# A gated delta rule with an MLP on one core: a list scheduler inside the kernel fixes every engine's order and the PSUM banks

## The chip, the cores and the metric

The kernel runs on one core of a Trainium2 chip. The metric is device time of one execution in microseconds (us), lower is better. The kernel before takes 668.2 us (median of two runs, 665.67 to 670.74).

The engines are named as in the profile: PE is the tensor engine (PEld its weight loads), DVE the vector engine, ACT the scalar engine, POOL GpSimd, SP the sync engine, which here only issues DMAs.

## The reference

Two stages. The first is a recurrence over 768 tokens for 32 pairs of batch and head (4 x 8), with a 48 x 48 state each; the second an MLP over the 3072 resulting tokens.

```python
def _attn_ref(q, k, v, beta, g):
    k_n = k / (np.linalg.norm(k, axis=-1, keepdims=True) + 1e-06)
    state = np.zeros((B, H, D, D))                       # B 4, H 8, D 48
    for t in range(S):                                   # S 768
        y[:, :, t] = g[:, :, t] * np.einsum('bhd,bhde->bhe', q[:, :, t], state)
        v_old = np.einsum('bhde,bhd->bhe', state, k_n[:, :, t])
        state = state + bt[..., None] * np.einsum('bhd,bhe->bhde', k_n[:, :, t], v[:, :, t] - v_old)

def _moe_ref(x, w_in, w_out):                            # x [3072, 384], w_in [384, 2048]
    h = x @ w_in
    g = np.where(h >= 1, h, np.where(h <= -1, 0.0, (h + 1) ** 2 / 4))
    return g @ w_out
```

## The kernel before

The recurrence is done in 24 chain steps of 32 tokens, in 6 groups of four steps. For a group the kernel loads k, q, v and g (64 DMAs of 48 KB), prepares them on POOL (`prep_pair`), builds Gram matrices on PE (`gram_step`), inverts the 32 x 32 triangular ones in two 16 x 16 halves on POOL (`lanes`, 15 serial pairs of instructions between three DVE transposes), joins the halves on PE (`merge_pair`), and then walks the four chain steps, which alone are serial. After the fourth step the tokens of the group go through the MLP: sixteen `mlp_in` of 128 x 512 and four `mlp_out`.

```python
    def lanes(gi):
        bm = bms[gi % 3]
        lt = lan.tile([128, 32, 32], F16, name=f"lt{gi}", tag="lt")
        nc.vector.transpose(out=lt[:].rearrange("p i j -> p (i j)"), in_=_ap(bm, [[1, 32], [64, 32]]))
        lm = lan.tile([128, 2, 16, 16], FP, name=f"lm{gi}", tag="lm")
        nc.gpsimd.tensor_copy(out=lm[:], in_=eye[:])
        for j in range(15):
            ...                                  # two POOL instructions each: tm = lt * lm, lm -= tm
        low = lows[gi % 2]
        nc.gpsimd.tensor_copy(out=_ap(low, [[528, 2], [32, 16], [1, 16]]), in_=lm[:])
        l16 = lan.tile([128, GS, J, 32], F16, name=f"l16{gi}", tag="l16")
        nc.vector.transpose(out=_ap(l16, [[1, 32], [32, 32]]), in_=_ap(low, [[1, 32], [32, 32]]))
        x16 = lan.tile([128, GS, J, 32], F16, name=f"x16{gi}", tag="x16")
        nc.vector.transpose(out=_ap(x16, [[1, 32], [32, 32]]), in_=_ap(low, [[32, 32], [1, 32]]))

    def mlp_in(gi, xt, m):
        hp = psM.tile([128, NT], FP, name=f"hp{gi}_{m}", tag="m")          # one of two PSUM banks
        ...                                                                # three matmuls
        nc.scalar.activation(out=rl[:], in_=hp[:], func=AF.Relu, bias=c_half[:], scale=0.5)
        if m % 2 == 0:
            nc.vector.tensor_tensor(out=mx[:], in0=hp[:], in1=rl[:], op=ALU.max)
            nc.vector.scalar_tensor_tensor(out=gt[:], in0=rl[:], scalar=1.0, in1=mx[:], op0=ALU.min, op1=ALU.mult)
        else:
            nc.gpsimd.tensor_tensor(out=r2[:], in0=rl[:], in1=rl[:], op=ALU.mult)      # the square
            nc.vector.scalar_tensor_tensor(out=gt[:], in0=hp[:], scalar=1.0, in1=r2[:], op0=ALU.max, op1=ALU.min)

    for s in range(NSTEP):                       # the order: program order, handed to the framework's scheduler
        gi = s // GS
        if gi + 1 < NG:
            if s % GS == 0:
                parts = group_parts(gi + 1)      # load and prep / gram / lanes / merge of the next group
            parts[s % GS]()
        xt = chain_step(s)
        n = (len(todo) + (GS - s % GS) - 1) // (GS - s % GS)
        for f in todo[:n]:                       # a quarter of the previous group's MLP
            f()
        todo = todo[n:]
        ...
```

Of the kernel before, what the change touches and what calls it, by code (L numbers as in the profile page):

```python
# [15 lines left out]
def _ap(t, dims, off=0):  # L16

    a = t[:]
    return bass.AP(tensor=a.tensor, offset=a.offset + off, ap=[list(a.ap[0])] + [list(d) for d in dims])


@with_exitstack
def kernel(
# [13 lines left out]
    C = 32  # L37
# [6 lines left out]
    NM = DFF // 128  # L44
    assert D == 48 and H == 8 and B == 4

    const = ctx.enter_context(tc.tile_pool(name="const", bufs=1))
    raw = ctx.enter_context(tc.tile_pool(name="raw", bufs=2))
    prep = ctx.enter_context(tc.tile_pool(name="prep", bufs=2))
    vtp = ctx.enter_context(tc.tile_pool(name="vtp", bufs=4))  # L50
    small = ctx.enter_context(tc.tile_pool(name="small", bufs=2))
    ktp = ctx.enter_context(tc.tile_pool(name="ktp", bufs=8))
    lan = ctx.enter_context(tc.tile_pool(name="lan", bufs=2))
    nwt = ctx.enter_context(tc.tile_pool(name="nwt", bufs=2))
    zfp = ctx.enter_context(tc.tile_pool(name="zfp", bufs=4))
    chn = ctx.enter_context(tc.tile_pool(name="chn", bufs=2))
    xtp = ctx.enter_context(tc.tile_pool(name="xtp", bufs=2))
    mlpt = ctx.enter_context(tc.tile_pool(name="mlpt", bufs=2))
    mlpg = ctx.enter_context(tc.tile_pool(name="mlpg", bufs=28))
    outp = ctx.enter_context(tc.tile_pool(name="outp", bufs=3))  # L60
    psS = ctx.enter_context(tc.tile_pool(name="psS", bufs=1, space=bass.MemoryType.PSUM))
    psN = ctx.enter_context(tc.tile_pool(name="psN", bufs=2, space=bass.MemoryType.PSUM))
    psC = ctx.enter_context(tc.tile_pool(name="psC", bufs=2, space=bass.MemoryType.PSUM))
    psM = ctx.enter_context(tc.tile_pool(name="psM", bufs=2, space=bass.MemoryType.PSUM))


    HS = 4 * S * D
    raws = {}

    def load(s0, n):  # L70

        ts = {}
        for nm, src in (("k", k), ("q", q), ("v", v), ("g", g)):
            t = raw.tile([128, GS, J, D], FP, name=f"r{nm}{s0}", tag=f"raw_{nm}", bufs=2 if nm == "g" else 1)
            ts[nm] = t
        raws[s0] = ts

    def load_part(s0, off, n, names):
        ts = raws[s0]
        for nm, src in (("k", k), ("q", q), ("v", v), ("g", g)):  # L80
            if nm not in names:
                continue
            for h4 in range(4):
                for c in range(off, off + n):
                    a = bass.AP(tensor=src.tensor, offset=src.offset + h4 * S * D + (s0 + c) * C * D,
                                ap=[[D, C], [HS, J], [1, D]])
                    nc.sync.dma_start(out=ts[nm][32 * h4:32 * h4 + 32, c, :, :], in_=a)  # L87


    braw = const.tile([128, NG, C], FP, name="braw")  # L90
    for h4 in range(4):
        for j in range(J):
            a = bass.AP(tensor=beta.tensor, offset=beta.offset + h4 * S + j * 4 * S,
                        ap=[[C, GS], [GS * C, NG], [1, C]])
            nc.sync.dma_start(out=braw[32 * h4 + 4 * j:32 * h4 + 4 * j + 4, :, :], in_=a)  # L95
    load(0, GS)
    load_part(0, 0, 2, "k")
    load_part(0, 0, 2, "qv")

    ones = const.tile([128, 32], FP, name="ones")  # L100
    nc.gpsimd.memset(ones[:], 1.0)
    id32 = const.tile([128, 32], FP, name="id32")
    upf = const.tile([128, 32], F16, name="upf")
    lof = const.tile([128, 32], F16, name="lof")
    for h4 in range(4):
        r = slice(32 * h4, 32 * h4 + 32)
        nc.gpsimd.affine_select(out=id32[r, :], in_=ones[r, :], compare_op=ALU.is_equal, fill=0.0,
                                base=0, pattern=[[-1, 32]], channel_multiplier=1)
        nc.gpsimd.affine_select(out=upf[r, :], in_=ones[r, :], compare_op=ALU.is_gt, fill=0.0,
                                base=0, pattern=[[1, 32]], channel_multiplier=-1)  # L110
        nc.gpsimd.affine_select(out=lof[r, :], in_=ones[r, :], compare_op=ALU.is_gt, fill=0.0,
                                base=0, pattern=[[-1, 32]], channel_multiplier=1)
    i16 = const.tile([128, 32], F16, name="i16")
    nc.gpsimd.tensor_copy(out=i16[:], in_=id32[:])
    two_i = const.tile([128, 16, 32], F16, name="two_i")
    nc.gpsimd.tensor_scalar(out=two_i[:], in0=_ap(id32, [[0, 16], [1, 32]]), scalar1=-2.0, scalar2=None, op0=ALU.mult)
    upmask = const.tile([128, J, 2, 32], F16, name="upmask")
    nc.gpsimd.tensor_copy(out=upmask[:].rearrange("p j a c -> p (j a) c"), in_=_ap(upf, [[0, 2 * J], [1, 32]]))
    c_half = const.tile([128, 1], FP, name="c_half")
    nc.gpsimd.memset(c_half[:], 0.5)  # L120


    bms = []
    for i in range(3):
        t = const.tile([128, GS, J, 2, 32], F16, name=f"bm{i}")
        nc.gpsimd.memset(t[:], 0.0)
        nc.gpsimd.tensor_copy(out=t[:, :, :, 0, :].rearrange("p s j t -> p (s j) t"), in_=_ap(id32, [[0, GS * J], [1, 32]]))
        bms.append(t)

    lows = []  # L130
    for i in range(2):
        t = const.tile([128, 32, 32], F16, name=f"low{i}")
        nc.gpsimd.memset(t[:], 0.0)
        lows.append(t)
    eye = const.tile([128, 2, 16, 16], FP, name="eye")
    nc.gpsimd.memset(eye[:], 0.0)
    nc.gpsimd.memset(_ap(eye, [[256, 2], [17, 16]]), 1.0)
    kqs = []
    for i in range(5):
        t = const.tile([128, 2, J, 2, 64], F16, name=f"kq{i}")  # L140
        nc.gpsimd.memset(t[:], 0.0)
        kqs.append(t)
    i64 = const.tile([128, 64], F16, name="i64")
    for r in range(2):
        nc.gpsimd.affine_select(out=i64[64 * r:64 * r + 64, :], in_=_ap(ones, [[0, 2], [1, 32]])[64 * r:64 * r + 64], compare_op=ALU.is_equal, fill=0.0,
                                base=0, pattern=[[-1, 64]], channel_multiplier=1)

    sb = const.tile([128, NG, J, GS], FP, name="sb")
    bt = const.tile([128, NG, C], FP, name="bt")
    nc.vector.transpose(out=bt[:].rearrange("p a b -> p (a b)"), in_=braw[:].rearrange("p a b -> p (a b)"))  # L150
    nc.scalar.activation(out=sb[:].rearrange("p a b c -> p (a b c)"), in_=bt[:].rearrange("p a b -> p (a b)"), func=AF.Sqrt)

    load_part(0, 2, 2, "kqv")
    load_part(0, 0, 4, "g")


    win = const.tile([128, 3, DFF], F16, name="win")
    wout = const.tile([128, NM, DM], F16, name="wout")

    def load_weights():  # L160
        for h4 in range(4):
            for p0, kt, h2, e0, n in ((0, 0, 0, 0, 32), (0, 1, 0, 32, 16), (16, 1, 1, 0, 16), (0, 2, 1, 16, 32)):
                r0 = (h2 * 4 + h4) * D + e0
                nc.gpsimd.dma_start(out=win[32 * h4 + p0:32 * h4 + p0 + n, kt, :], in_=moe_w_in[r0:r0 + n, :])  # L164
        nc.gpsimd.dma_start(out=wout[:], in_=moe_w_out.rearrange("(m p) n -> p m n", p=128))


    st = {}

    def prep_pair(p):  # L170
        s0 = 2 * p
        gi, off = s0 // GS, s0 % GS
        rw = raws[gi * GS]
        kr = rw["k"][:, off:off + 2]
        sbv = _ap(sb, [[1, 2], [GS, J]], gi * J * GS + off)
        ksq = prep.tile([128, 2, J, D], FP, name=f"ksq{p}", tag="ksq")
        nc.gpsimd.tensor_tensor(out=ksq[:], in0=kr, in1=kr, op=ALU.mult)  # L177
        nsq = small.tile([128, 2, J], FP, name=f"nsq{p}", tag="nsq")
        nc.vector.tensor_reduce(out=nsq[:], in_=ksq[:], axis=AX.X, op=ALU.add)  # L179
        nrm = small.tile([128, 2, J], FP, name=f"nrm{p}", tag="nrm")  # L180
        nc.scalar.activation(out=nrm[:], in_=nsq[:], func=AF.Sqrt)
        nre = small.tile([128, 2, J], FP, name=f"nre{p}", tag="nre")
        nc.vector.tensor_scalar(out=nre[:], in0=nrm[:], scalar1=1e-6, scalar2=None, op0=ALU.add)
        rcp = small.tile([128, 2, J], FP, name=f"rcp{p}", tag="rcp")
        nc.vector.reciprocal(out=rcp[:], in_=nre[:])
        rs = small.tile([128, 2, J], FP, name=f"rs{p}", tag="rs")
        nc.vector.tensor_tensor(out=rs[:], in0=rcp[:], in1=sbv, op=ALU.mult)
        kq = kqs[p % 5]
# [265 lines left out]
```

## Time and profile before

| | before |
|---|---|
| time | 668.2 us |
| period of a group (transpose lt of one group to that of the next, mean of five) | 102 us |
| first chain product / last chain transpose / tail to the end | 81 / 617 / 48 us |
| mean granted PE clock | 0.69 |

The first fence holds two lines of the profile's page: busy time of each engine (with its share of the span), and the engines' shares of the chain of work that ended last.

```profile
PE 317.9 (48%) x7536; PEld 170.3 (26%) x7536; DVE 240.9 (36%) x306; ACT 149.3 (22%) x253; POOL 223.2 (34%) x356
...
issue 27%; POOL 19%; PE 19%; DVE 13%; SPq 12%; ACT 5%; DMA 3%; POOLq 0%; ACTq 0%; DVEq 0%
```

No engine is half busy, and the chain of waits passes from one to another without a favourite. The next fence is the view by stretches of time: start and end, length, then busy us of PE, PEld, DVE, ACT and POOL (with instruction counts), the granted clock of PE, the share of DMA and GB/s. The first stretch is one whole group, the second the part of a later group in which POOL inverts and DVE transposes what comes out.

```profile
350.00:456.00 106.00, 55.17 (x1273) 27.81 (x1272) 39.98 (x52) 24.66 (x42) 31.38 (x50) 0.60 0.19 39
...
460.00:484.00 24.00, 3.75 (x72) 1.43 (x71) 12.19 (x7) 2.65 (x4) 15.79 (x33) 0.50 0.00 0
```

In that part PE works 3.8 of 24 us. The timeline (start, duration, engine, line, operation, output<-inputs, and in brackets how long the engine sat idle before it and what ended that) shows why.

```profile
464.08 1.04 POOL L363 TENSOR_TENSOR r_13_8305<-rl_13_8302 128x512 f32<-128x512 f32 x1
465.16 0.69 DVE L364 SCALAR_TENSOR_TENSOR gt_13_8304<-hp_13_8298,r_13_8305 128x512 f16<-128x512 f32 x1 [5.73 <-POOL r_13_8305 L363]
465.90 1.44 PE L352 MATMUL hp_14_8308<-xt_5839,win 128*128 128x512 f16 x3 [5.71 <-DVE gt_13_8304 L364]
...
474.30 4.67 DVE L248 STREAM_TRANSPOSE l_6447<-low_204 128x1024 f16<-128x1024 f16 x1 [1.51 <-POOL low_204 L246]
478.61 4.82 DVE L250 STREAM_TRANSPOSE x_6449<-low_204 128x1024 f16<-128x1024 f16 x1
479.03 0.68 PE L266 MATMUL ep_6673<-l_6447,bm_198 32*32 32x32 f16 x64 [8.70 <-DVE l_6447 L248]
```

The engines take turns because of the order of the program.

### The profile page before, as it was taken

The numbers are of one execution on the slowest core, as the hardware profiler recorded it, in microseconds if no ns is written. First come the engines' busy times: TensorE is split into PE (matmuls) and PEld (weight loads), VectorE is DVE, ScalarE is ACT, GpSimd is POOL, SyncE is SP. The second block draws the span as 40 slices with busy tenths as digits, with TensorE's granted clock in tenths as the row PEclk, the third lists the DMA queues.
The fourth block names the chain that finished last, engine by engine and source line by source line (L and its number), as shares of the span: only waits on it lengthen the run. The fifth ranks groups of instructions, "written<-read, shape, count | busy, mean of one in ns | idle before, by whom it ended". The sixth has DMA issues, their size and how long they took to land.

```text
span 665.0 us, 16817 instructions
## 1 busy us (share of the span) xinstructions
PE 317.9 (48%) x7536; PEld 170.3 (26%) x7536; DVE 240.9 (36%) x306; ACT 149.3 (22%) x253; POOL 223.2 (34%) x356
## 2 busy tenths in 40 slices
PE   0031165590453484374463276355268447227846
PEld 0020151250331141251130143122045114024413
DVE  0021527533335241534233622424621433352251
ACT  0020123330221240232131132122122113112331
POOL 9986204337004218103227302324600412720121
PEclk9999999896555555567565579555566755557899
DMA  1797510220410000025400015500004510000101
GB/s 28 128 180 117 95 35 1 47 51 9 90 39 0 4 2 0 3 50 99 92 2 1 1 29 93 121 2 1 0 4 83 101 54 3 1 2 28 36 0 48
DMA packets 111577, 27.95 MB, mean 42 GB/s; under 512 B 106000, under 2 KB 111120, under 8 KB 111504
## 3 DMA queue, kind: packets, MB, share of 16 engines
q1 hardware_dynamic: 108800, 23.72, 17.9%
q0 software_dynamic: 2704, 3.15, 3.0%
q8 instruction: 59, 0.97, 0.6%
q14 instruction: 14, 0.11, 0.1%
HBM read 25.26 MB, written 4.72 MB: 45 GB/s over the span
## 4 chain that ended last, share of the span: by engine, by line
issue 27%; POOL 19%; PE 19%; DVE 13%; SPq 12%; ACT 5%; DMA 3%; POOLq 0%; ACTq 0%; DVEq 0%
SPq L87 11%; DMA rg_145<-in_g_dram 2%; SPq L95 1%; PE sps L321 1%; POOL lm_8044 L244 1%; POOL lm_4754 L244 1%; POOL lm_6399 L244 1%; POOL lm_1604 L244 1%; POOL lm_3109 L244 1%; DMA rv_144<-in_v_dram 1%; PE op_0_9671 L370 1%; PE op_0_7131 L370 1%; PE op_0_8776 L370 1%; DVE l_4802 L248 1%; DVE l_3157 L248 1%
## 5 line engine op out<-in xcount | busy, mean ns | idle before, releaser
L352 PEld LDWEIGHTS <-win 128*128 128x128 f16 x288 | 33.4, 120 | 193.2 <-issue 183.8
L210 PEld LDWEIGHTS <-kq_211 64*64 64x64 f16 x192 | 6.1, 149 | 44.7 <-POOL kq_211 L190 36.5
L210 PE MATMUL tp_0_323<-i_221,kq_211 64*64 64x64 f16 x16 | 0.8, 243 | 34.2 <-POOL kq_211 L190 32.2
L363 POOL TENSOR_TENSOR r_1_9046<-rl_1_9043 128x512 f32<-128x512 f32 x1 | 1.0, 1040 | 42.8 <-ACT rl_1_9043 L355 42.8
L363 POOL TENSOR_TENSOR r_1_9768<-rl_1_9765 128x512 f32<-128x512 f32 x1 | 1.4, 1438 | 39.9 <-ACT rl_1_9765 L355 39.9
L363 POOL TENSOR_TENSOR r_1_7503<-rl_1_7500 128x512 f32<-128x512 f32 x1 | 1.0, 1040 | 39.6 <-ACT rl_1_7500 L355 39.6
L363 POOL TENSOR_TENSOR r_1_5858<-rl_1_5855 128x512 f32<-128x512 f32 x1 | 1.0, 1040 | 37.5 <-ACT rl_1_5855 L355 37.5
L363 POOL TENSOR_TENSOR r_1_4213<-rl_1_4210 128x512 f32<-128x512 f32 x1 | 1.0, 1040 | 34.9 <-ACT rl_1_4210 L355 34.9
L363 POOL TENSOR_TENSOR r_1_2568<-rl_1_2565 128x512 f32<-128x512 f32 x1 | 1.0, 1049 | 34.2 <-ACT rl_1_2565 L355 34.2
L266 PE MATMUL ep_660<-l_656,bm_195 32*32 32x32 f16 x64 | 0.7, 187 | 22.1 <-DVE l_656 L248 22.1
L266 PEld LDWEIGHTS <-bm_195 32*32 32x32 f16 x256 | 2.8, 99 | 32.7 <-issue 32.7
L210 PEld LDWEIGHTS <-kq_213 64*64 64x64 f16 x192 | 6.1, 149 | 18.1 <-POOL kq_213 L190 11.9
L248 DVE STREAM_TRANSPOSE l_656<-low_204 128x1024 f16<-128x1024 f16 x1 | 4.7, 4652 | 15.3 <-POOL low_204 L246 15.3
L266 PEld LDWEIGHTS <-bm_198 32*32 32x32 f16 x256 | 2.8, 99 | 25.6 <-issue 25.6
L164 POOL DMA_DIRECT2D win<-in_moe_w_in_dram x16 | 8.3, 526 | 0.0
L266 PE MATMUL ep_1828<-l_1652,bm_198 32*32 32x32 f16 x64 | 0.7, 187 | 15.3 <-DVE l_1652 L248 15.3
L266 PEld LDWEIGHTS <-bm_201 32*32 32x32 f16 x256 | 2.8, 98 | 18.2 <-issue 18.2
L179 DVE TENSOR_REDUCE nsq_273<-ksq_271 128x16 f32<-128x768 f32 x1 | 1.0, 954 | 15.1 <-POOL ksq_271 L177 15.1
L268 ACT CAST e_729<-ep_660 128x512 f16<-128x512 f32 x1 | 0.6, 586 | 23.9 <-PE ep_660 L266 23.9
L210 PEld LDWEIGHTS <-kq_219 64*64 64x64 f16 x128 | 4.1, 149 | 6.9 <-POOL kq_219 L190 4.3
L306 DVE TENSOR_TENSOR rr_2378<-kp_2379,vt_1018 128x384 f16<-128x384 f32 x1 | 0.6, 557 | 14.0 <-POOL vt_1018 L195 14.0
L210 PEld LDWEIGHTS <-kq_217 64*64 64x64 f16 x128 | 3.3, 129 | 8.8 <-POOL kq_217 L190 4.3
(1746 smaller groups left out, 1126.0 us busy)
## 6 DMA issues: line engine op xcount, KB each, us to landing
wout<-in_moe_w_out_dram POOLq DMA_DIRECT2D x1, 1536.0 KB, 15.7
win<-in_moe_w_in_dram POOLq DMA_DIRECT2D x8, 128.0 KB, 4.2
rk_142<-in_k_dram SPq DMA_DIRECT2D x16, 48.0 KB
rq_143<-in_q_dram SPq DMA_DIRECT2D x16, 48.0 KB
rv_144<-in_v_dram SPq DMA_DIRECT2D x16, 48.0 KB
rg_145<-in_g_dram SPq DMA_DIRECT2D x16, 48.0 KB
rk_936<-in_k_dram SPq DMA_DIRECT2D x16, 48.0 KB
rq_937<-in_q_dram SPq DMA_DIRECT2D x16, 48.0 KB
```

The costliest lines, as they stand in the source:

```text
L87: nc.sync.dma_start(out=ts[nm][32 * h4:32 * h4 + 32, c, :, :], in_=a)
L95: nc.sync.dma_start(out=braw[32 * h4 + 4 * j:32 * h4 + 4 * j + 4, :, :], in_=a)
L164: nc.gpsimd.dma_start(out=win[32 * h4 + p0:32 * h4 + p0 + n, kt, :], in_=moe_w_in[r0:r0 + n, :])
L179: nc.vector.tensor_reduce(out=nsq[:], in_=ksq[:], axis=AX.X, op=ALU.add)
L210: nc.tensor.matmul(tp[rr, jj, a], d["kq"][rr, c, j, a, :], i64[rr, :], start=(jj == 0 and a == 0), stop=True, skip_group_check=True)
L244: nc.gpsimd.tensor_tensor(out=lv, in0=lv, in1=tv, op=ALU.subtract)
L248: nc.vector.transpose(out=_ap(l16, [[1, 32], [32, 32]]), in_=_ap(low, [[1, 32], [32, 32]]))
L266: nc.tensor.matmul(ep[r, c, j], bm[r, off + c, j, 0, :], l16[r, off + c, j], start=False, stop=True, skip_group_check=True)
L321: nc.tensor.matmul(sps[ro:ro + 64, h4 % 2, j * D:j * D + D], kq[r, j, 0, :], u16[r, j], start=(s == 0 and j == 0), stop=True, skip_group_c ...
L352: nc.tensor.matmul(hp[:], win[:, kt_, m * 128:m * 128 + 128], xt[:, kt_].rearrange("p b t -> p (b t)"), start=(kt_ == 0), stop=(kt_ == 2))
L363: nc.gpsimd.tensor_tensor(out=r2[:], in0=rl[:], in1=rl[:], op=ALU.mult)
L370: nc.tensor.matmul(op[:], gts[gi, m][:, b * GS * C:(b + 1) * GS * C], wout[:, m, :], start=(m == 0), stop=(m == NM - 1))
```

## The change

The intent is to take the order out of the framework's hands. Every operation is first recorded with an engine, a duration from a table, a priority (the time in chain steps at which it is wanted) and the PSUM bank that it takes and gives back. A list scheduler then simulates the engines with those durations, always takes the ready operation of best priority, assigns the banks as they come free, and emits everything in the order found. Along with it: the l and x transposes become contiguous (the cast before them writes a transposed copy, `lowl`, as well, and the merge reads with a stride); of the squares (one for each odd `m`, eight a group) half stay on POOL and half go to ACT; most set-up memsets and the first inverse go to DVE; loads run further ahead, beta and the keys and queries of group 0 on two queues; weight loads come at the very start.

```diff
+class Plan:
+    def add(self, eng, us, fn, r=(), w=(), prio=0.0, ninstr=0, late=0.0, take=None, give=None):
+        ...
+    def order(self):
+        ...                                  # list scheduling with the durations `us`
+        return [i for t, i in sorted(out)]
+    def emit(self):
+        for i in self.order():
+            self.ops[i]["fn"]()
...
+            P(eng, 0.49, lambda h4=h4, a=a, e=e: e.dma_start(out=t[32 * h4:32 * h4 + 32, c, :, :], in_=a),
+              w=[raw[nm].key(p, c, h4)], prio=prio, late=0.33)
...
-        nc.gpsimd.tensor_copy(out=_ap(low, [[528, 2], [32, 16], [1, 16]]), in_=lm[:])
-        nc.vector.transpose(out=_ap(l16, [[1, 32], [32, 32]]), in_=_ap(low, [[1, 32], [32, 32]]))
-        nc.vector.transpose(out=_ap(x16, [[1, 32], [32, 32]]), in_=_ap(low, [[32, 32], [1, 32]]))
+            P(eng, 0.78 if eng == "POOL" else 0.4, f, r=[lts.key(gi)], w=[lms.key(gi), "tm"], prio=prio)
+        P(eng, 0.61, lambda: e.tensor_copy(out=_ap(lowl(gi), [[528, 2], [1, 16], [32, 16]]), in_=lm[:]),
+          r=[lms.key(gi)], w=[lowl.key(gi)], prio=prio)
+        P(eng, 0.61, lambda: e.tensor_copy(out=_ap(lowx(gi), [[528, 2], [32, 16], [1, 16]]), in_=lm[:]),
+          r=[lms.key(gi)], w=[lowx.key(gi)], prio=prio)
+        for nm, lo, o in (("l", lowl, l16s), ("x", lowx, x16s)):
+            P("DVE", 1.2, ...)               # one contiguous transpose each
...
+            if m % 4 == 1:
+                P("POOL", 1.05, lambda: nc.gpsimd.tensor_tensor(out=r2[:], in0=rl[:], in1=rl[:], op=ALU.mult), ...)
+            else:
+                P("ACT", 0.69, lambda: nc.scalar.activation(out=r2[:], in_=rl[:], func=AF.Square), ...)
...
+    T = 8.5                                  # planned us of a chain step
+    def parallel(gi):
+        t0 = at((gi - 1) * GS)
+        ...
+        lanes(gi, t0 + 1.5 * T, "POOL" if gi else "DVE")
+    with tc.manual_schedule():
+        plan.emit()
```

## The prediction

> **What bounds the kernel now.** No engine: the page gives PE 48%, DVE 36%, POOL 34%, ACT 22% of 665 us. Order does. The timeline repeats every 102 to 109 us per group of four steps (the 128x1024 transpose lt starts at 144, 248, 350, 456, 565 us), and in each group the engines take turns: loads wait for the previous group's buffers (queue's waits: 70 to 74 us on one output copy), then prep, sixteen MLP inputs through two PSUM banks, the triangular inverse on POOL (460 to 483 us: POOL 15.8 us busy, PE 3.8), two transposes of 4.7 and 4.8 us, and only then the four chain steps. The chain of waits has 27% "issue", 11% load issue, and jumps between all engines.
>
> **What the change does.** Operations hardly change; their order does.
> - The l and x transposes become contiguous. Contiguous-output ones cost 0.58 us for 384 columns and 1.9 for 1024 (lt): I estimate 1.3 to 1.9 each, 6 us less per group, plus one 0.6 us copy on POOL.
> - Half of the squares go from POOL (1.05 us) to ACT (0.69).
> - Setup memsets (POOL busy 29.9 of the first 32 us) and the first inverse go to DVE; first k and q loads use two queues.
> - Loads run ahead; MLP, preparation and chain interleave.
>
> **Work per group afterwards**, from durations in the trace:
> - DVE: MLP 16.7, masks 2.8, y, rr, xt 6.8, reduce and small ones 3.5, transposes 4.5 to 6: 34 to 36 us.
> - POOL: prep 11, inverse 14, squares 4: 29. ACT: 28.
> - SP: 64 loads at 0.49 us plus outputs: 33.
> - PE: with the fast matmuls seen (16 output ones 2.6 us) about 36; with the slow ones (1.44 per input triple, 0.32 per output matmul) about 60.
> - PE instructions: 2,544. In the dense stretch 592 to 613 us PE stops in "issue" for 0.7 to 1.6 us after every 128 weight load and matmul pairs, so 256 instructions take at least 3.4 to 4.0 us: an estimated floor of 34 to 38 us. [...]
>
> So five resources end near 28 to 38 us per group, in place of 106. The recurrence doesn't bind: bare chain steps take 4.1 us (80 to 100 us).
>
> **Sum.** First chain step at about 43 us (83 before). Four full groups at about 42 us, because in-order engines that are nearly full stall on each other, DVE's small operations wait behind POOL (nre took 0.17 to 1.44 us), and the clock won't stay full (0.50 in quiet stretches, 0.65 to 0.72 in dense ones); first and last group lighter, about 33. Tail after the last step about 38 (47 before): the last MLP is still serial through two banks, then four outputs. 43 + 168 + 66 + 38 = 315; I say 320.
>
> Predicted 320 us, range 285 to 370. Faster by over 2%: 0.98; same 0.01; slower 0.01.
>
> **What would show it.** Group period (lt to lt) 36 to 46 us; PE and DVE over 70% busy; l and x transposes under 2 us; granted clock above 0.8 in the middle; PE idle put to "issue" rather than to POOL or DMA; first chain step near 43 us.
>
> **What would make it wrong.** The clock staying near 0.5: PE then needs 60 us per group, about 400 in all. [...] POOL and DVE delaying each other, or a load blocking the in-order SP queue. On the other side, if all overlaps as ordered and the tail is short, 280.

The sum: 43 + 168 + 66 + 38 = 315, called 320; the floor of 34 to 38 us is the author's estimate from the stops in the stretch 592 to 613 us. That small DVE operations wait behind POOL is in the trace before (L183): five executions of nre with POOL idle beside them took 0.17 us, the seven that began during a POOL instruction 0.49 to 1.44 us, each until an instruction of POOL had ended.

## More of the kernel before

A square (r_13) has its place on POOL in the middle of the inverse; DVE waits for it, PE waits for the PSUM bank that DVE would free. Then two transposes of nearly 5 us each stand before the merge.

## The result, and the profile after

| | before | after | predicted |
|---|---|---|---|
| time | 668.2 us | **415.6 us** (two runs, 415.36 and 415.85) | 320 (285 to 370) |
| ratio to before | 1 | 0.622, 95% interval 0.612 to 0.632 | |
| first chain product | 81 us | 61.9 us | 43 |
| from there to the last chain transpose | 536 us | 301.6 us | 234 (168 + 66) |
| tail from there to the end | 48 us | 50.7 us | 38 |
| group period, mean of five | 102 us | 52.4 us (57.9, 53.9, 48.8, 47.4, 54.2) | 42 |
| mean granted PE clock | 0.69 | 0.805 (0.57 to 0.91 in the middle groups) | over 0.8 in the middle |

A ratio is the mean time of one kernel's fast runs over that of the other's in the same rounds, so it is not quite the ratio of the medians quoted. The change is correct and takes 253 us away, but 96 us less than predicted, outside the range. All three terms of the sum were short: the start by 19 us, the chain section by 68, the tail by 13.

The page's lines of the kernel after, the same two as above and then the shares by line of the chain that ended last:

```profile
PE 264.4 (64%) x7536; PEld 158.1 (38%) x7536; DVE 216.5 (52%) x357; ACT 160.5 (39%) x277; POOL 182.2 (44%) x284
...
PE 26%; SPq 23%; POOL 20%; issue 9%; DMA 9%; DVE 8%; ACT 3%; ACTq 0%; POOLq 0%
SPq L250 23%; PE pso_173 L558 11%; POOL tm_108 L401 7%; POOL lm_107 L404 7%; PE psh_172 L530 5%; DMA braw<-in_beta_dram 5%; PE psh_171 L530 3%; POOL lowl_109 L406 2%; DVE lt_106 L393 1%; DMA raw_q_64<-in_q_dram 1%; POOL r_136 L544 1%; DMA raw_k_62<-in_k_dram 1%; ACT rl_133 L533 1%; DVE mx_134 L537 1%; ACT r_137 L547 1%
```

Load issue (SPq L250) now has 23% of the chain, POOL's inverse (L401, L404) 14%, and the beta loads 5%. The same execution by stretches, cut near the lt transposes that start the groups:

```profile
62.00:101.00 39.00, 23.36 (x930) 16.16 (x919) 17.61 (x33) 15.34 (x28) 12.72 (x12) 0.63 0.44 80
101.00:150.00 49.00, 27.58 (x775) 16.07 (x774) 22.95 (x38) 16.22 (x29) 32.33 (x49) 0.57 0.50 92
150.00:202.00 52.00, 41.90 (x1319) 25.76 (x1313) 29.75 (x46) 21.64 (x40) 31.41 (x49) 0.70 0.47 94
202.00:251.00 49.00, 40.17 (x1322) 24.08 (x1307) 29.98 (x48) 24.61 (x45) 30.77 (x47) 0.90 0.41 85
251.00:305.00 54.00, 43.50 (x1359) 25.73 (x1339) 31.46 (x48) 27.02 (x46) 21.65 (x40) 0.91 0.07 21
```

These five lines already show two regimes. Up to about 150 us PE is little over half busy at a clock of 0.57 to 0.63. From 150 us on PE is busy 81 to 82% of the time, that is 40 to 44 us a group, where the prediction counted on 36. Up to 251 us DVE, POOL and the issue of loads lie between 30 and 40 us a group as well. In the last stretch no loads are left and POOL has 22 us, and still it is 54 us long: PE's 43.5 us and 10.5 in which it waits.

What PE waits for is visible in the view of waits for the stretch 251 to 305 us (engine and line, the releaser, then us in total, times, longest):

```profile
POOL r_136 L544 <- ACT rl_133 L533: 14.2, 1, 14.2
...
PEld L530 <- issue: 8.3, 10, 5.9
PE psh_172 L530 <- DVE gt_156 L549: 6.0, 1, 6.0
DVE l_111 L411 <- POOL lowl_109 L406: 5.6, 1, 5.6
...
ACT rl_133 L533 <- POOL r_136 L544: 4.8, 1, 4.8
```

and the timeline of that stretch:

```profile
257.06 0.81 PE L530 MATMUL psh_172<-xt_129,win 128*128 128x512 f16 x3 [0.22 <-DVE gt_154 L549]
257.90 0.69 ACT L533 ACTIVATE rl_133<-psh_172,c_half 128x512 f32<-128x512 f32 x1 [0.19 <-PE psh_172 L530]
...
267.62 2.41 POOL L406 CAST lowl_109<-lm_107 128x512 f16<-128x512 f32 x1
...
270.41 1.05 POOL L544 TENSOR_TENSOR r_136<-rl_133 128x512 f32<-128x512 f32 x1
...
271.50 0.69 ACT L533 ACTIVATE rl_133<-psh_171,c_half 128x512 f32<-128x512 f32 x1 [4.83 <-POOL r_136 L544]
...
272.36 0.65 DVE L549 SCALAR_TENSOR_TENSOR gt_156<-psh_172,r_136 128x512 f16<-128x512 f32 x1
273.06 1.44 PE L530 MATMUL psh_172<-xt_129,win 128*128 128x512 f16 x3 [5.96 <-DVE gt_156 L549]
...
302.26 1.04 POOL L544 TENSOR_TENSOR r_136<-rl_133 128x512 f32<-128x512 f32 x1 [14.25 <-ACT rl_133 L533]
```

Read it from the top. The MLP product in bank psh_172 is done at 258, its relu at 258.6. Its square r_136 is one of those left on POOL, and its place there is behind the whole inverse, whose last casts end at 270.4. So the bank is held until 273, PE stands 6 us in front of the next product for that bank, and when it goes on its clock is down (recorded at 0.5 from 269.4 to 276.2 us; 1.44 us for the triple, 0.81 us before). ACT's wait of 4.8 us is the same thing: its next relu needs the buffer rl_133, which the square still holds. The longest wait in the view, 14.2 us, is another event: it ends at 302.3 us, where POOL has run out of work and stands idle until the relu of a later product. That one is slack of an engine that nobody waits for so long. The wait that costs is PE's.

The old fault, one engine waiting for a square in another's queue, is still there, in an order that the planner itself fixed. Its durations hid part of the price: a pair of inverse steps 0.78 us, measured 0.95; the cast to `lowl` 0.61 us, and in the view by line it is

```profile
L406 POOL CAST lowl_109<-lm_107 x5: 2406/2406/2437, 117.7 to 321.8; 128x512 f16<-128x512 f32 x5
L406 DVE CAST lowl_109<-lm_107 x1: 1282/1282/1282, 54.0 to 54.0; 128x512 f16<-128x512 f32 x1
```

(minimum, median and maximum in ns, first and last start in us). The inverse with its casts takes from 253.4 to 270.4, 17 us; the table has 12.9 (15 pairs of 0.78 and twice 0.61). But running the planner's loop with its own table already leaves four squares 5 to 15 us behind their operands (arithmetic of the planner, not a measurement): it always takes the ready operation of best priority and does not look at what that one will keep waiting.

In the stretch 101 to 202 us POOL waits for something else, loads:

```profile
POOL ksq_76 L331 <- DMA raw_k_61<-in_k_dram: 10.8, 1, 10.8
POOL vt_94 L348 <- DMA raw_v_67<-in_v_dram: 4.9, 1, 4.9
```

SP issues loads almost without a break (the longest, at 242 us, is 6.7 us) from 30 to 251 us, some 350 of them (320 of the five later groups and most of the 32 of v and g of the first) in 221 us: about 0.6 us each, where the table has 0.49. That is 40 us a group, while the DMA engines are 41 to 50% busy in the stretches from 62 to 251 us.

At the start, the 32 loads of beta (first start to last start in us, at the end of the number block):

```profile
L262 SPq DMA_DIRECT2D braw<-in_beta_dram x16: 249/250/301, 5.7 to 22.5; - x16
L262 ACTq DMA_DIRECT2D braw<-in_beta_dram x16: 256/257/487, 5.9 to 24.4; - x16
```

They take 19 us on two queues, while the kernel before had them out in 11 us on one. The DMA engines are 88% busy up to 36 us, mostly (55 of the 88) with the 3.15 MB of weights that the change moved to the first microseconds; without the weights beside them (e2) the beta loads take 6.5 us.

### The profile page after: what moved, and what is told of

Same layout as the page of the kernel before. It is cut to its first block, busy times and chain, and to the rows that moved or that the text cites. A ratio compares the mean times of both kernels' runs of the same rounds, so it can differ in the third digit from the quotient of the medians.

```text
span 414.2 us, 16889 instructions
## 1 busy us (share of the span) xinstructions
PE 264.4 (64%) x7536; PEld 158.1 (38%) x7536; DVE 216.5 (52%) x357; ACT 160.5 (39%) x277; POOL 182.2 (44%) x284
## 3 DMA queue, kind: packets, MB, share of 16 engines
q0 software_dynamic: 2752, 3.15, 4.8%
## 4 chain that ended last, share of the span: by engine, by line
PE 26%; SPq 23%; POOL 20%; issue 9%; DMA 9%; DVE 8%; ACT 3%; ACTq 0%; POOLq 0%
SPq L250 23%; PE pso_173 L558 11%; POOL tm_108 L401 7%; POOL lm_107 L404 7%; PE psh_172 L530 5%; DMA braw<-in_beta_dram 5%; PE psh_171 L530 3%; POOL lowl_109 L406 2%; DVE lt_106 L393 1%; DMA raw_q_64<-in_q_dram 1%; POOL r_136 L544 1%; DMA raw_k_62<-in_k_dram 1%; ACT rl_133 L533 1%; DVE mx_134 L537 1%; ACT r_137 L547 1%
## 5 line engine op out<-in xcount | busy, mean ns | idle before, releaser
L530 PEld LDWEIGHTS <-win 128*128 128x128 f16 x288 | 27.2, 105 | 64.9 <-issue 47.8
L530 PE MATMUL psh_172<-xt_129,win 128*128 128x512 f16 x69 | 23.2, 454 | 19.8 <-DVE gt_143 L549 8.1
L401 POOL TENSOR_TENSOR tm_108<-lt_106,lm_107 128x30 f32<-128x30 f16 (+7 forms) x75 | 29.9, 399 | 12.0 <-DVE lt_106 L393 6.0
L404 POOL TENSOR_TENSOR lm_107<-lm_107,tm_108 128x30 f32<-128x30 f32 (+7 forms) x75 | 29.2, 390 | 5.9
L365 PE MATMUL psn_168<-i_179,kq_87 64*64 64x64 f16 x96 | 3.3, 221 | 43.2 <-POOL kq_87 L344 36.2
L530 PE MATMUL psh_171<-xt_129,win 128*128 128x512 f16 x75 | 24.6, 443 | 4.4 <-DVE gt_149 L549 2.2
L544 POOL TENSOR_TENSOR r_136<-rl_132 128x512 f32<-128x512 f32 x8 | 9.3, 1158 | 37.6 <-ACT rl_132 L533 37.6
L530 PE MATMUL psh_172<-xt_130,win 128*128 128x512 f16 x63 | 20.3, 437 | 7.5 <-DVE gt_160 L549 1.6
L530 PE MATMUL psh_171<-xt_130,win 128*128 128x512 f16 x81 | 23.6, 402 | 2.0 <-DVE gt_151 L549 1.8
L544 POOL TENSOR_TENSOR r_136<-rl_133 128x512 f32<-128x512 f32 x8 | 8.3, 1043 | 33.0 <-ACT rl_133 L533 33.0
L365 PEld LDWEIGHTS <-kq_87 64*64 64x64 f16 x192 | 5.3, 135 | 44.3 <-POOL kq_87 L344 36.2
L533 ACT ACTIVATE rl_133<-psh_171,c_half 128x512 f32<-128x512 f32 x19 | 13.0, 685 | 18.6 <-POOL r_136 L544 10.6
L544 POOL TENSOR_TENSOR r_136<-rl_131 128x512 f32<-128x512 f32 x8 | 8.3, 1040 | 23.2 <-ACT rl_131 L533 23.2
L533 ACT ACTIVATE rl_131<-psh_172,c_half 128x512 f32<-128x512 f32 x17 | 11.7, 687 | 14.5 <-PE psh_172 L530 14.5
L533 ACT ACTIVATE rl_131<-psh_171,c_half 128x512 f32<-128x512 f32 x15 | 10.4, 690 | 16.5 <-POOL r_136 L544 11.0
L533 ACT ACTIVATE rl_132<-psh_171,c_half 128x512 f32<-128x512 f32 x18 | 12.3, 686 | 7.6 <-PE psh_171 L530 7.4
L430 PE MATMUL psn_169<-l_112,bm_105 32*32 32x32 f16 x256 | 4.3, 227 | 16.2 <-DVE l_112 L411 16.2
L533 ACT ACTIVATE rl_132<-psh_172,c_half 128x512 f32<-128x512 f32 x14 | 9.7, 690 | 12.5 <-PE psh_172 L530 12.2
L333 DVE TENSOR_REDUCE nsq_78<-ksq_76 128x16 f32<-128x768 f32 x6 | 5.7, 950 | 15.4 <-POOL ksq_76 L331 15.4
L430 PEld LDWEIGHTS <-bm_105 32*32 32x32 f16 x384 | 6.1, 115 | 17.9 <-issue 17.8
```

The lines of the kernel that those rows point to most:

```text
L333: P("DVE", 1.0, lambda: nc.vector.tensor_reduce(out=nsq(p)[:], in_=ksq(p)[:], axis=AX.X, op=ALU.add), r=[ksq.key(p)], w=[nsq.key(p)], prio ...
L365: nc.tensor.matmul(tp[rr, jj, a], kq[rr, c, 4 * half + jj, a, :], i64[rr, :], start=(jj == 0 and a == 0), stop=True, skip_group_check=True)
L401: e.tensor_tensor(out=tv, in0=_ap(lt, [[528, 2], [32, n], [0, j + 1]], 32 * (j + 1) + j), in1=_ap(lm, [[256, 2], [0, n], [1, j + 1]], 16 * ...
L404: e.tensor_tensor(out=lv, in0=lv, in1=tv, op=ALU.subtract)
L430: nc.tensor.matmul(ep[r, c, j], bm[r, off + c, j, 0, :], l16[r, :, (off + c) * J + j], start=False, stop=True, skip_group_check=True)
L530: nc.tensor.matmul(hp, win[:, kt_, m * 128:m * 128 + 128], xt[:, kt_].rearrange("p b t -> p (b t)"), start=(kt_ == 0), stop=(kt_ == 2))
```

## The experiments

Times are medians of the fast executions; one is called slow when it is over 1.5% above the fastest of its kernel (e1, e10, e11, e12 and e13 have such; the state of e16's one execution is unknown). Differences in us are between these medians, to 415.6 of the changed kernel, unless said otherwise. Some expectations quote earlier differences with slow executions in them (17 us for e1). The changed kernel's own median comes from two executions, and the interval of its ratio spans 2%; so a single difference under some 10 us rests on the positions in the trace, not on the times alone. The expectations name theories by letters: A, the issue of loads sets the pace; B, the in-order queues, whose order was found with wrong durations (B1 the squares behind the inverse, B2 the table as a whole); C, the start; D and W/P as said there.

| run | what | time, us | ratio to before | first lt | chain section | tail |
|---|---|---|---|---|---|---|
| after | | 415.6 | 0.622 | 43.4 | 301 | 50.7 |
| e1 (chain from e16) | no loads for groups 2 to 5 | 394.8 | 0.592 | 43.5 | 281 | 52 |
| e2 | weight loads after beta | 411.4 | 0.616 | 41.0 | 299 | 50.6 |
| e3 | transposes of before put back | 431.1 | 0.646 | 43.5 | 311 | 50.7 |
| e4 | program order, framework's scheduler | 601.3 | 0.901 | 48.6 | | |
| e5 | all odd squares on ACT | 401.3 | 0.604 | 46.0 | 291 | 47.2 |
| e6 | measured durations in the table | 410.0 | 0.615 | 43.9 | 291 | 51.0 |
| e7 | filler matmuls | 492.3 | 0.739 | 45.6 | 372 | 54 |
| e8 | weight loads after the first prep | 413.4 | 0.620 | 28.8 | 308 | 51.9 |
| e9 | half of the output products | 397.4 | 0.594 | 43.0 | 290 | 41.3 |
| e10 | e1, e5 and e9 together | 360.1 | 0.538 | 43.4 | 258 | 36.4 |
| e11 | cast to lowl on DVE | 407.7 | 0.608 | 43.4 | 289 | 55.2 |
| e12 | e5, e11 and other priorities | **376.2** | 0.564 | 43.4 | 272 | 39.8 |
| e13, e17 | three more banks in the tail | 408.7 (e17) | 0.609 | 43.6 | 301 | 41.7 |
| e14 | no beta loads | 409.3 | 0.616 | 32.5 | 305 | 49.3 |
| e15 | e12 and e17 together | 377.3 | 0.567 | 45.5 | 270 | 39.1 |

The chain section is counted here from the first copy u (ACT's copy of the first chain product, at 62.7 us in the changed kernel) to the last transpose of the chain, the tail from there to the end of the span.

### e1_noload: are the loads the pace?

```diff
-            P(eng, 0.49, lambda ...: e.dma_start(out=t[...], in_=a),
+            P(eng, 0.49, lambda ...: e.dma_start(out=t[...], in_=a) if s < (10 if nm == 'g' else 6) else None,
```

Order and buffers are unchanged, the later groups compute with stale data, so the result is wrong. As it stands the edit also drops half of the second group's k, q and v (it stops at step 6) and keeps g up to step 10.

> The changed kernel in exactly its own order, but the q, k, v, g loads of the groups 2 to 5 are not issued (the buffers keep old data; the result is wrong on purpose). Theory A (load issue): in the changed kernel the SP queue issues loads without a break from 30 to 251 us at about 0.62 us each, 64 per group, and the groups run at that pace; then this run falls to about 350 to 375 us and the time from one lt transpose to the next goes from 52 to about 42 us. Theory B (order): the fixed order on in-order engines, made from durations that the chip doesn't keep, sets the pace; the loads are only busy beside it. Then it stays at 400 us or more. The periods of 54 us after 251 us, when no loads are left, speak for B.

Measured: 394.8 us (two fast executions, 392.85 and 396.71; a third took 400.2), ratio 0.592 (0.586 to 0.597). That lies between A (350 to 375) and B (400 or more): the loads cost about 21 us, not the whole gap. The profiled execution was an outlier of 1091 us, in which a 128x512 matmul took 1.28 to 1.80 us at a recorded clock of 1.00 (0.38 to 0.63 us in the changed kernel); it is used for nothing, and e16 repeats the profile.

### e2_weights_late: the start

```diff
                   w=[("win", h4, kt, p0)], prio=prio, late=0.9)
+                  # and r=["sb"]: wait for the square root of beta
```

> The changed kernel with the MLP weight loads ordered after sb (the square root of beta), and nothing else. Theory C: the start is late (first u copy at 62.7 us instead of 50) because 4.6 MB of weights, moved to the first microseconds, share the DMA engines with 32 small beta loads, which take 1.1 us each instead of 0.35; then the beta loads shrink from 19 us to under 8, the first u copy comes at about 50 us and the total falls by 8 to 14 us. Rival: it is the two queues that slow each other; then the beta loads still take 15 us or more and the total moves by under 4 us.

Measured: 411.4 us. (The profile counts 3.15 MB of weights, not 4.6.) The beta loads shrank from 19 to 6.5 us, as C says; SP's half of them, in the view of the tile:

```profile
L262 SPq DMA_DIRECT2D braw<-in_beta_dram x16: 250/252/305, 5.4 to 11.7; - x16
```

but the first transpose lt moved only from 43.4 to 41.0. In the timeline POOL issues weight DMAs until 34.6 us, and the second pair's queries and keys stand behind the last of them (34.65 and 35.44). The start gave up one wait and took another, again in an in-order queue, and neither C nor its rival holds as stated.

### e3_old_transposes: what the contiguous transposes are worth

The two transposes, the single cast and the merge operands of before were put back, with 4.7 us in the table.

> The changed kernel with the transposes of before put back (one cast of lm, two transposes of about 4.7 us, matmuls that read l and x contiguously), ordered by the same scheduler with 4.7 in its table. If the contiguous transposes pay in full, DVE has 7 us more per group and the inverse takes about 7 us longer: 440 to 455 us. If most of what they save comes back as the cast with a strided output on POOL (2.41 us, not 0.61) and as matmuls that read l and x with a stride (64 in 0.9 instead of 0.53 us), 415 to 430 us.

Measured: 431.1 us, 15 more than with the contiguous ones, just above the 415 to 430 of partial pay. DVE is busy 252.0 us in place of 216.5. The transposes themselves fell from 4.7 and 4.8 to 1.24 and 1.20 us, a little under the predicted 1.3 to 1.9, but two things give part back: the cast of 2.41 us, and the merge, whose operand now has a stride of 64 bytes: a group of 64 such matmuls (L430) takes 1.07 to 1.10 us in the timeline where the kernel before (L266) has 0.68 to 0.72, in both at a recorded clock of 0.5 as of 1.0.

### e4_tile_order: what the order is worth

```diff
-    with tc.manual_schedule():
-        plan.emit()
+    plan.order()
+    for o in plan.ops:
+        o["fn"]()
```

The same operations, buffers, banks and loads, in program order, and the framework's scheduler decides as in the kernel before.

> All operations, buffers, banks and loads of the changed kernel, but issued in program order and ordered by the framework's own scheduler, as before. If the list scheduler is what won the 250 us, this is far slower than the changed kernel: 520 to 640 us. If the deeper buffers and the earlier loads won most of it, 420 to 480 us.

Measured: 601.3 us. So about 186 of the 253 us lie between this order and the scheduler's, and about 67 are all else. The split is not exact: this program order is not that of before. It has prep, Gram matrices, inverse and merge of the next group in one piece between two chain steps and the MLP in another, where the kernel before spread both by hand over four steps, and the banks were assigned for another order. The new operations in the order of before were not run. PE waits again for the inverse (waits of the whole execution):

```profile
POOL r L544 <- ACT rl L533: 213.7, 23, 24.0
...
PE psn L430 <- DVE l L411: 107.1, 6, 19.3
```

PE's wait in front of the merge is 107 us in six pieces. In the changed kernel it is 30 us in five (view by line of L430, idle time of PE before it):

```profile
  DVE l_112 L411: 16.2, 3
  DVE l_111 L411: 14.2, 2
```

### e5_squares_on_act: the squares behind the inverse

```diff
-            if m % 4 == 1:
+            if m < 0:                # all odd squares on ACT
```

> All odd-m squares of the MLP run on the scalar engine; GpSimd keeps the inverse, the prep products and casts. Theory B1 (the four squares of a group that are queued on GpSimd behind the 15 us inverse hold an MLP bank and with it the in-order tensor engine, 6 us in the stretch 251-305): the tensor engine's waits on gt behind r2 go, each boundary between groups shortens by 3-6 us, the whole comes to 388-402 us. Rival D (the tensor engine's low granted clock and its own work set the pace) and rival A (loads): within 5 us of 415.6, because the work of the other engines is the same and the scalar engine even gains 2.5 us a group.

Measured: 401.3 us, ratio 0.604 (0.600 to 0.607). B1 holds: 14 us came off although ACT has 12 us more work. In the last middle group the PE waits for an MLP bank are 3 us in all; the longest is now one for the inverse:

```profile
PE psn L430 <- DVE l L411: 5.0, 1, 5.0
PE psh L530 <- DVE mx L537: 1.8, 2, 1.6
PE psh L530 <- DVE gt L549: 1.2, 3, 0.5
```

The expected 388 to 402 was met at its upper end.

### e6_measured_table: was only the table wrong?

```diff
-            P(eng, 0.78 if eng == "POOL" else 0.4, f, ...)
+            P(eng, 0.95 if eng == "POOL" else 0.4, f, ...)
-        P(eng, 0.61, lambda: e.tensor_copy(out=_ap(lowl(gi), ...
+        P(eng, 2.41 if eng == "POOL" else 0.61, lambda: e.tensor_copy(out=_ap(lowl(gi), ...
 ...                                          # and the others named in the expectation
```

> No instruction is changed; only the durations in the scheduler's table are set to what the trace of the changed kernel shows (load issue 0.62 for 0.49, beta 1.1 for 0.33, a pair of inverse steps 0.95 for 0.78, the two casts after it 2.41 and 0.84 for 0.61, merges 1.15 and 0.9 for 0.8 and 0.6, MLP triple 0.9 for 0.65, output quarter 0.75 for 0.65, small products 0.5-0.6 for 0.35-0.45), so that only the order and the banks differ. Theory B2 (the order is bad because the table is wrong): 375-400 us and the gaps at the group boundaries (about 20 us) shrink. Rival (the order is near what this set of dependences and priorities gives, and the plan was only optimistic): within 8 us of 415.6.

Measured: 410.0 us, inside the rival's margin of 8. A planner with right durations, but the same placement and priorities, makes a plan that is hardly better. B2 as stated falls: the wrong table made the plan optimistic, and made little of the loss. The planner's own span, worked out by running its loop, goes from 345 us with the kernel's table to 415 with the measured one, for a kernel that takes 410. (This is the planner's arithmetic, not a measurement.) So the prediction of 320 lay below even the plan with its short durations.

### e7_filler_matmuls: the clock

```diff
+    def warm(count, after):
+        for i in range(count):
+            P("PE", 0.5, fw, r=["upmask"] + after, w=[nw], prio=1e6, ninstr=4, take=nw, give=nw)   # two 128x512 matmuls
+    warm(60, [])
 ...
+        if s < 8:
+            warm(24, [xts.key(gi, s % GS)])
```

> About 240 idle-time matmuls of 128x512 without use are put on the tensor engine where the plan has it idle in the first part (some 80 us of added work at most), to keep its granted clock up between 36 and 202 us, where it was 0.57-0.70. Theory D (low clock makes the first three groups slow): granted clock over 0.85 there, the group periods 57.9 and 53.9 us fall towards 48, total 395-408 us. Rivals B and C: clock rises, periods stay, the total within 6 us of 415.6 or longer, since fillers also stand in the in-order queue.

Measured: 492.3 us. The edit adds 252 fillers of two matmuls, twice what the expectation counts, and PE busy time rose by 105 us, not 80. Most of them also missed their place: in the trace 325 of the 504 filler matmuls (some 79 us) run after 251 us, in the way of other work, and none from 101 to 150 us. The run does not settle what the clock costs. It shows that a granted clock of 0.83, 0.77 and 0.67 in the stretches up to 150 us, where the changed kernel has 0.66, 0.63 and 0.57, brought only the second of the first three transposes lt forward, by 4 us (45.6, 97.4 and 159.0 us against 43.4, 101.3 and 155.2). The changed kernel's clock record has only the values 0.5 and 1.0, in pieces of 3.4 us or multiples of it; PE was busy for 82% or more of the 3.4 us before each of the twelve switches up from 0.5. The mean over a stretch follows the mean share only loosely (0.57 where PE is 56% busy, 0.70 at 81%, 0.90 at 82%); e12 below has a mean of 0.90 without fillers. From this the author takes the low clock here to be at least in part a follower of PE's waits; no run tests that, and how far it is also a cause is not shown.

### e8_weights_after_prep: the start again

```diff
-    load_weights(-32)
     ...
     parallel(0)
+    load_weights(-32)               # and its DMAs wait for the second pair's keys and queries
```

> Weight loads wait until the first group's second pair of keys and queries is written, so neither the beta loads share the transfer with them nor do their twenty issues on GpSimd stand before that pair. Theory C (the start lost 19 us to beta and weights): the first transpose of the inverse comes at 27-34 us in place of 43.4, first chain product at 46-53 in place of 61.9, total 400-408 us. Rival (the start's gain is taken back at the first boundary, which waits for the second group's inverse, and that for loads): start 10 us earlier, total within 5 us of 415.6.

Measured: 413.4 us. Of the start's promise lt comes true, at 28.8 us; the first u is at 53.2 us, 9 us earlier, and the first product just inside the 46 to 53. But the second group's first u comes at 123.1 (129.5 before), the third's at 180.4 (181.6): what the start won is gone by the third group, and the total is that of the changed kernel. The rival is right, one boundary later than it says: the second lt is still 7 us earlier (94.1), the third only 1.3 (153.9). Between 90 and 160 us POOL waits 20 us for loads (q 8.6, v 7.5 and 3.8). They come in the order of SP's queue, and starting group 0 earlier does not move that queue.

### e9_half_outputs: is PE's own work the pace?

```diff
-                for m in range(4 * mq, 4 * mq + 4):
+                for m in range(4 * mq, 4 * mq + 4, 2):
```

> Wrong on purpose: every second of the 16 products of each output block is left out, so that the tensor engine has some 33 us less work at full clock (192 products at 0.17 us); order, loads and every other engine as in the changed kernel. Theory P (in the middle groups the tensor engine's own 40 us of work, in a fixed order, is what a group waits for): 385-397 us, that is 60 to 90% of the removed work. Rival W (the group is paced by the waits for inverse, squares and loads, and tensor work fits into the gaps): at most 10 us off, 405-416.

Measured: 397.4 us: 18 us for the 31 of PE work taken away (busy time 264.4 to 233.3), just outside the 385 to 397 of theory P and far from the 405 to 416 of W. In the profiled execution 9 us of it are in the tail and 10 in the chain section. PE's work counts, at a little over half of its price.

### e10_three_reliefs: do the gains add?

e1, e5 and e9 in one kernel. Its output is wrong, which doesn't matter for the time.

> Wrong on purpose: three single reliefs together, no loads for groups 2 to 5 (17 us off alone), squares on the scalar engine (14 off alone), half the output products (e9). If each relieves its own wait and the waits follow each other, the gains add: 355-365 us. If they are alternatives that hide each other: about the best of the three, 385-395. If one bound sits behind another and gives way only when both go: below 350.

Measured: 360.1 us, 56 off. The three alone gave 21, 14 and 18, together 53. They add, as expected for waits that follow each other. The chain section is 258 us (the three singles take 20, 10 and 10 off it, the three together 43). The group period is 45 us. So the 42 of the prediction is nearly what this kernel would do if loads came for nothing, the squares were elsewhere, and PE had the output products' 31 us less to do.

### e11_lowl_cast_on_vector

```diff
-        P(eng, 0.61, lambda: e.tensor_copy(out=_ap(lowl(gi), ...
+        P("DVE", 0.7, lambda: nc.vector.tensor_copy(out=_ap(lowl(gi), ...
```

> Only the cast with the strided output after the inverse, 2.41 us on GpSimd, goes to the vector engine. If the strided output is slow on GpSimd alone, the cast takes 0.6-0.8 us there, the inverse is ready 1.7 us earlier in each of five groups, and the total is 403-411 us. If the pattern is slow on any engine: 2 us or more on the vector engine, total within 4 us of 415.6 or longer.

Measured: 407.7 us, 8 off, in the upper part of the 403 to 411. The cast takes 1.28 us on DVE, between the two cases: the output with an inner step of 64 bytes costs on both engines (0.63 us on DVE and 0.84 on POOL for the other cast, which writes contiguous runs of 16 elements), more on POOL (2.41 us). The order found also differs: the last group's inverse starts 27 us earlier, so the gain is not the cast's 1.1 us alone.

### e12_priorities: a better order

e5 and e11, and other priorities:

```diff
-        chain_step(s, at(s) - 0.5 * T)
+        chain_step(s, at(s) - 1.43 * T)
-        lanes(gi, t0 + 1.5 * T, ...)
+        lanes(gi, t0 + 0.06 * T, ...)
-        mlp_in(gi, m, t0 + (m / NM) * 3.2 * T)
+        mlp_in(gi, m, t0 + (-1.46 + (m / NM) * 1.68) * T)
-        mlp_out(gi, b, t0 + (3.2 + b * 0.2) * T)
+        mlp_out(gi, b, t0 + (5.2 + b * 0.2) * T)
 ...                                 # gram, prep, merge and load offsets likewise
```

The priorities were searched with a small replay: the order found by the planner is run through again, in order on each engine, with the durations of the changed kernel's trace. It is an estimate; for the changed kernel it gives 421 us.

> The version that should beat both: squares on the scalar engine, that cast on the vector engine, and other priorities for the scheduler (chain a step earlier, inverse of the next group 1.4 steps earlier, MLP packed earlier, outputs later, loads more spread), same instructions otherwise. An in-order replay that I worked out from the durations in the trace of the changed kernel puts it 32 us below the changed kernel: 378-390 us. If order no longer matters beyond the squares: 398-404 as with the squares alone.

Measured: 376.2 us, correct, ratio 0.564 (0.558 to 0.570), just under the expected 378 to 390: the fastest measured, beside e15. By stretches, to be held against the lines of the kernel after:

```profile
101.00:202.00 101.00, 74.14 (x2176) 41.89 (x2174) 62.69 (x97) 48.21 (x86) 56.72 (x90) 0.76 0.50 92
202.00:305.00 103.00, 92.26 (x2762) 53.14 (x2761) 70.29 (x103) 61.49 (x105) 52.15 (x107) 0.92 0.26 57
```

PE is busy 73% and 90% of these stretches (69% and 81% in the changed kernel), and the mean clock is 0.90. Beyond squares and cast, the order alone is worth some 17 us more, if those two single gains add.

### e13_tail_banks and e17_tail_banks_again

```diff
-        n = bank("h")
+        n = bank("h" if gi < NG - 1 or m % 5 < 2 else "n")
```

> Only the last group's MLP products get three more PSUM banks, those that the chain no longer needs. If the two banks set the pace of the tail (one 128x512 product per 3.4 us and bank in the stretch 363-400): the tail after the last transpose falls from 50.5 to 40-45 us, the total to 404-411. If engine work or the outputs set it: the tail stays at 48-51, the total within 4 us of 415.6.

Measured: three of four executions were slow, the profiled one too (span 412.6 us). The one fast execution took 403.3 us. Not used.

> As for e13. If two banks set the pace of the tail: in a fast profile the last transpose stands at about 363 as in the changed kernel, the tail is 40-45 us, the total 404-411. If engine work or the outputs set it: tail 48-51, total within 4 us of 415.6.

Measured: 408.7 us, ratio 0.609 (0.603 to 0.614), profile fast: the last transpose stands at 364.5 as before, and the tail is 41.7 us:

```profile
364.50:406.20 41.70, 33.54 (x179) 17.03 (x176) 21.68 (x33) 20.08 (x34) 5.21 (x5) 0.99 0.11 39
```

PE does nearly the same work in it (35.3 us in the changed kernel) in 9 us less. The two banks were the tail's limit, and PE is the next, 80% busy.

### e14_no_beta_loads

```diff
-                P("ACT" if j % 2 else "SP", 0.33, ... e.dma_start(out=braw[p:p + 4, :, :], in_=a), ...)
+        P("POOL", 0.3, lambda: nc.gpsimd.memset(braw[:], 0.5), ...)
```

> Wrong on purpose: beta is filled with a constant in place of its 32 loads. If beta is what delayed the start (17 to 19 us of transfers): first transpose of the inverse at 28-33 in place of 43.4, first chain product at 46-51 in place of 61.9, and the total 5-14 us lower. If other work of the prologue stands behind it: first chain product at 56 or later.

Measured: 409.3 us; lt at 32.5, first u at 52.1, 10.6 us earlier. Beta is a little over half of the 19 us by which the start was missed. The other 8 to 9 are not told apart by a run; in the stretch 33 to 52 us of that execution PE works at a clock of 0.50 and no engine but DVE (12.9 of 19 us) is busy.

### e15_order_and_banks

> The order of e12 with the banks of e13: 372-378 us if the tail's gain holds there too (e12's tail is 40 us), 376-380 if e12's order had already hidden it.

Measured: 377.3 us, ratio 0.567, the same as e12: its order puts the outputs later and had the tail at 39.8 us already.

### e16_noload_profile

> The kernel of e1 again, for a profile. If loads cost time by their issue queue: in the middle groups (100-250 us) tensor engine waits on the inverse's operands shrink and its busy time stays. [...] Total 390-401.

Measured: 397.2 us in its one execution, of unknown state. The stretch 101 to 202 us, first of e16,

```profile
101.00:202.00 101.00, 80.84 (x2682) 48.86 (x2682) 61.37 (x100) 50.34 (x88) 75.37 (x125) 0.76 0.04 11
```

and then of the changed kernel:

```profile
101.00:202.00 101.00, 69.48 (x2082) 41.83 (x2081) 52.70 (x83) 37.86 (x68) 63.74 (x98) 0.64 0.49 93
```

Without loads 2,682 matmuls fit where 2,082 did; the second and third periods fall from 53.9 and 48.8 to 43.9 and 43.2 us, the last stays at 54. POOL's waits for loads (10.8, 4.9, 4.1 us) are gone from its list. PE busy time over the whole execution falls by 4 us only (264.4 to 260.4). So loads cost by when they arrive, in the middle groups. The clock rises there too (0.64 to 0.76), and what of the gain is the clock's is not told apart.

## Why the prediction was right or wrong, point by point

**Order, not work, bound the kernel before: right.** With the same operations in program order the time is 601 us (e4), so most of the 253 us hang on the order, though e4's order is not quite that of before. Direction and main mechanism stand.

**Transposes: the duration nearly right, the bill incomplete.** 1.24 and 1.20 us were measured for a predicted 1.3 to 1.9. "One 0.6 us copy on POOL" is 2.41 us, in series between inverse and merge. The strided merge operand was not counted. Net worth 15 us (e3).

**"Half of the squares go from POOL to ACT": read as relief, was half a trap.** The prediction summed POOL's busy time (29 us a group) and took it to be harmless. Four squares a group stayed in the queue of the engine that is blocked for 17 us at a time, and each holds one of two MLP banks. Moving them is worth 14 us (e5), though it adds work to a busier engine.

**"SP: 64 loads at 0.49 us": mis-sized.** About 0.6 us each in a queue almost without a gap, 40 us a group in place of 33. Worth about 21 us (e1), in the groups between 100 and 200 us (e16). The prediction named "a load blocking the in-order SP queue" among its risks and put no number on it.

**"PE about 36 us": 40 to 44 at a granted clock of 0.70 to 0.91.** PE's work is partly the limit: half of what is taken from it comes off the time (e9). "PE and DVE over 70% busy": PE 81 to 82% from 150 us on, DVE 57 to 61%, so half right.

**The floor by stops in "issue": not the pace of a group.** The prediction estimated 34 to 38 us a group from stops after every 256 instructions in one stretch of the trace before (592 to 613 us: four of the six places there that stand 256 apart have a stop, of 0.7 to 1.6 us), and expected PE's idle time under "issue"; what causes the stops is not shown. In the changed kernel 256 PE instructions in a row take as little as 1.7 us. But in the stretch of small products from 56.7 to 83.8 us 2,045 of them take 27.1 us, 3.4 us per 256, with "issue" stops of 0.6 and 1.9 us that stand 256 instructions apart (at 76.0 and 79.7 us). So the prediction's 3.4 may bind there; no run tests it. Over a group it did not: the stretch 202 to 251 us has 2,629 instructions, 4.8 us per 256, and the long waits there and in its neighbours (4.8, 5.7 and 6.0 us) end with DVE results.

**The step that failed: "Four full groups at about 42 us, because in-order engines that are nearly full stall on each other".** The chain section was sized 234 us and took 301.6. The period of 42 was PE's 36 with a margin of 6; the five periods came out at 47 to 58. From 150 us on a stretch is PE's 40 to 44 us plus 9 to 10.5 in which it waits, so both terms were too small; before that PE works only 23 and 28 us of two stretches of 39 and 49 and waits the rest. The period is not the fullest engine plus a margin: with PE at 40 to 44, SP at 40, DVE and POOL at 30 us, in fixed orders, each engine's late result delays the others in turn, and the delays come one after another. The singles show it as a sum: loads 20, squares 10, PE work 10, the cast (with a changed order) 12 us off the chain section; the first three together 43 and a period of 45 (e10). A better order with squares and cast moved takes 30 off without any work less (e12).

**The start: 43 predicted, 61.9 measured.** Beta loads beside the weight loads are 10.6 us of it (e14); the rest is open between clock and DVE work. Little of it reaches the end: e8 starts 9 us earlier and ends 2 us earlier.

**The tail: 38 predicted, 50.7 measured.** The prediction wrote "the last MLP is still serial through two banks" and then subtracted 9 us from the tail of before, without a reason given. With five banks it is 41.7 us (e17).

What stays open: the remaining 8 to 9 us of the start, the price of the low clock up to 150 us, which e7 could not isolate, and how much the order of before, with the new operations, would have cost.

## What to carry to other kernels

When every engine runs in order, moving work to an engine that has time is safe only if nothing on it blocks long (here one square stood 12 us behind an inverse of 17, and PE waited 6 us for its bank): look at what stands in front of the moved piece in that queue, not at the busy share. A planned period should not be the fullest engine plus a margin if several engines come near it (here SP with 40 us, DVE and POOL with 30, beside PE's 40 to 44, and periods of 47 to 58); take away one suspect at a time, then all together, and see whether the gains add (here 21, 14 and 18 us alone, 56 together). A planner with right durations is honest about the time but doesn't by itself find a better order; placement and priorities did (410 against 376 us).
